# Moving first-level adds and norm transposes of a pre-norm transformer block onto DMA

## The chip, the cores and the metric

The kernel runs on one core of one Trainium2 chip. The metric is the device time of one execution in microseconds (us). A single execution scatters by about one per cent, so every variant was run several times, in rounds with the kernel before on the same chip. An execution is called fast when it is within 1.5% of the fastest of the same kernel; only fast ones enter the comparisons.

The engines are called PE (TensorE matmul), PEld (TensorE weight load, which overlaps PE), DVE (VectorE), ACT (ScalarE), POOL (GpSimd) and SP (SyncE). A name such as SPq means the engine's own instruction queue, from which it issues DMAs one after the other.

## The reference

One pre-norm block on 2048 rows of width 512: local dilated attention (32 heads of 16, eight shifts with a stride of two rows), then a gated ReLU feed-forward part (width 1376), each with a residual.

```python
def _A_ref(x, wqkv, wo):                 # H = 32, Dh = 16, W = 8, dil = 2
    q, k, v = ...(x @ wqkv)...           # each [B, H, S, Dh]
    idx = pos[:, None] - (jnp.arange(W) * dil)[None, :]
    kg, vg = k[..., idx, :], v[..., idx, :]
    logits = einsum("bhsd,bhswd->bhsw", q, kg) * Dh ** -0.5   # masked where idx < 0
    o = einsum("bhsw,bhswd->bhsd", softmax(logits), vg)       # the sum over eight shifts
    return merge_heads(o) @ wo

def _B_ref(x, W_gate, W_up, W_down):
    return (relu(x @ W_gate) * (x @ W_up)) @ W_down

h  = x + _A_ref(_layernorm(x), A_wqkv, A_wo)
out = h + _B_ref(_layernorm(h), B_W_gate, B_W_up, B_W_down)
```

## The kernel before

The 2048 rows are worked in four chunks (0 to 3) of 512 rows, each of four blocks of 128 rows. A chunk has two norms: the first (called x) feeds the q, k, v products, the second (called h) feeds the up and gate products. So there are eight norm outputs. Each is transposed before its products. A small planner in the kernel orders all operations: each has an engine, a planned duration, a planned extra latency and a rank from a tuned list, and every engine then executes its operations strictly in the planned order.

The parts that the change touches are these. A norm's output is transposed by TensorE, four 128x128 squares for a block, and ScalarE copies the result out of PSUM (the tiles called bank in the traces). A branch by DMA is there but not used:

```python
PESUM = ()
DMAT = ()                       # (norm, chunk) pairs to be transposed by DMA
RPE, OPE = (0,), ()             # chunk 0: attention residual added by TensorE (identity matmul)
...
if (ln, tk) in DMAT:
    for j in range(lo, hi):                 # a block of 128 rows
        xn, a = norm(j)
        def f_td(j=j, xn=xn):
            for t in range(NT):             # NT = 4 squares of 128x128
                nc.sync.dma_start_transpose(out=dst.t[:, t, j * P:(j + 1) * P],
                                            in_=xn.t[:, t * P:(t + 1) * P])
        evs.append(add((ln + "td" + gk, tk), "SP", 2.0, f_td, [a], pr,
                       take=[dst], use=[xn], lat=2.5))
    continue
...
def f_tp(j=j, j0=j0, xn=xn, tp=tp):         # the way by TensorE
    for t in range(NT):
        o = t * 2 * P + (j - j0) * P
        nc.tensor.transpose(tp.t[:].bitcast(BF16)[:, o:o + P],
                            xn.t[:, t * P:(t + 1) * P], identity[:])
```

The sum over the eight shifts is a tree on VectorE: eight weighted copies of v in one buffer, then halves are added three times.

```python
def f_a(n, mt):
    V.tensor_tensor(out=mt.t[:, 0:n, :], in0=mt.t[:, 0:n, :], in1=mt.t[:, n:2 * n, :], op=ALU.add)
...
m = add(("mu%d" % t, tk), "DVE", D40, f_mu, ...)      # the eight weighted copies
for n, du in ((4, D20), (2, D10), (1, D2)):
    f = lambda n=n, mt=mt, f=f_a: f(n, mt)
    if n == 1 and tk in EARLY: ...                    # last add writes the attention output
    else:
        m = add(("tree%d" % t, tk), "DVE", du, f, [m], tpr, use=[mt], lat=0.03)
```

The softmax here doesn't subtract the row's maximum and nothing guards it: scores larger than these inputs give would overflow.

## Time and profile before

| | before |
|---|---|
| time, median of 3 runs | 208.53 us (208.37 to 210.53) |
| span of the profiled execution | 206.6 us |
| TensorE, VectorE, ScalarE busy | 96%, 79%, 68% |
| GpSimd busy | 1% |

The page gives two more lines. The first is the clock that was granted to TensorE, in tenths, one digit for each fortieth of the span. The second is the chain of work that ended last, as shares of the span by engine.

```profile
PEclk9999999999999999999999999999999999999999
...
PE 64%; DVE 20%; issue 5%; DMA 4%; ACT 4%; SPq 1%; DVEq 0%
```

The clock never dips, and DMA hardly stands in the chain: only the first loads do. The timeline of SP at the start (start us, us, engine, line, operation, tile) has the row of issues. The last line is from the view of the stores' source line (issues in ns: least, median, most):

```profile
1.65 0.43 SPq L265 DMA_DIRECT2D wq_sb<-in_A_wqkv_dram  x1
2.12 0.51 SPq L265 DMA_DIRECT2D wv_sb<-in_A_wqkv_dram  x1
...
L773 SPq DMA_DIRECT2D out_dram<-row x17: 332/332/382, 103.1 to 204.3; - x17
```

These are plain copies from and to HBM, the chip's main memory. No transposing and no accumulating DMA runs in this kernel.

### The profile page before, as it was taken

The page shows a single profiled execution, that of the slowest core. Times are in us where ns is not written, and L with a number is a line of the kernel's source. Part 1 is how long each engine was busy: PE and PEld are TensorE (multiplying, and loading weights), DVE is VectorE, ACT ScalarE, POOL GpSimd, SP SyncE. Part 2 cuts the span into 40 slices and gives each one's busy share as a digit, 9 for nine tenths or more (in the row PEclk, how much of TensorE's full clock was granted, in tenths as well). Part 3 has the DMA queues.
Part 4 walks back from the last instruction along what each step waited for, and adds up shares of the span by engine and source line. Part 5 has one row for each costly group of instructions (what it writes and reads, how often), then busy time and mean ns, then how long its engine had stood idle before and what let it go on. Part 6 is the DMA issues. An engine that isn't in the chain of part 4 may idle for free.

```text
span 206.6 us, 2992 instructions
## 1 busy us (share of the span) xinstructions
PE 197.8 (96%) x1139; PEld 97.6 (47%) x1159; DVE 162.3 (79%) x241; ACT 140.6 (68%) x277; POOL 1.8 (1%) x14
## 2 busy tenths in 40 slices
PE   8697998999999999999999999999999999999994
PEld 8563444455543334444444444454444445444452
DVE  6579999999999999998889998659998564011414
ACT  3659989989899996749588557465465553535800
POOL 3000000000000000000000000000000000000000
PEclk9999999999999999999999999999999999999999
DMA  6999900000000000000010000001000000200003
GB/s 199 340 381 407 302 12 0 0 0 3 0 0 0 3 0 0 0 0 3 2 51 0 3 0 27 25 3 51 0 0 23 28 3 31 70 0 0 3 0 102
DMA packets 8813, 10.70 MB, mean 52 GB/s; under 512 B 512, under 2 KB 7648, under 8 KB 8800
## 3 DMA queue, kind: packets, MB, share of 16 engines
q1 hardware_dynamic: 7984, 9.73, 13.7%
q10 hardware_dynamic: 816, 0.79, 1.1%
q8 instruction: 9, 0.15, 0.3%
q14 instruction: 4, 0.03, 0.0%
HBM read 8.42 MB, written 2.10 MB: 51 GB/s over the span
## 4 chain that ended last, share of the span: by engine, by line
PE 64%; DVE 20%; issue 5%; DMA 4%; ACT 4%; SPq 1%; DVEq 0%
PE bank L721 37%; PE bank L758 19%; DVE big L549 7%; PE bank L683 5%; DMA x_sm<-in_A_x_dram 4%; DVE big L637 4%; DVE big L640 4%; DVE st L390 3%; ACT big L622 2%; PE bank L456 2%; ACT row L422 1%; PE bank L555 1%; ACT quad L510 1%; DVE quad L644 1%; PE bank L616 1%
## 5 line engine op out<-in xcount | busy, mean ns | idle before, releaser
L721 PE MATMUL bank<-quad,wu_sb 128*128 128x512 bf16 (+1 forms) x176 | 41.8, 379 | 0.1
L721 PE MATMUL bank<-quad,wg_sb 128*128 128x512 bf16 (+1 forms) x169 | 41.4, 379 | 0.3
L758 PE MATMUL bank<-wd_sb,gT 128*128 128x512 bf16 (+3 forms) x183 | 40.2, 366 | 0.2
L728 ACT ACTIVATE gr<-bank 128x512 bf16<-128x512 f32 (+1 forms) x44 | 25.8, 608 | 15.7 <-PE bank L721 10.9
L549 DVE TENSOR_TENSOR big<-quad,kT 128x4096 bf16<-128x4096 bf16 x16 | 35.9, 2279 | 0.1
L637 DVE TENSOR_TENSOR big<-big,vT 128x4096 bf16<-128x4096 bf16 x16 | 35.9, 2280 | 0.0
L725 ACT CAST up_sb<-bank 128x512 bf16<-128x512 f32 (+1 forms) x44 | 25.4, 589 | 14.3 <-PE bank L721 9.2
L640 DVE TENSOR_TENSOR big<-big 128x2048 bf16<-128x2048 bf16 (+2 forms) x36 | 30.5, 888 | 0.1
L741 DVE TENSOR_TENSOR gT<-gr,up_sb 128x1024 bf16<-128x1024 bf16 (+1 forms) x24 | 15.2, 639 | 18.4 <-ACT up_sb L725 11.6
L721 PEld LDWEIGHTS <-wg_sb 128*128 128x128 bf16 (+1 forms) x176 | 17.5, 100 | 20.6 <-issue 0.4
L721 PEld LDWEIGHTS <-wu_sb 128*128 128x128 bf16 (+1 forms) x176 | 17.5, 100 | 20.7 <-issue 0.8
L758 PEld LDWEIGHTS <-gT 128*128 128x128 bf16 (+1 forms) x187 | 17.8, 98 | 19.0 <-issue 0.9
L622 ACT CAST big<-bank 128x512 bf16<-128x512 f32 x32 | 16.8, 620 | 2.1 <-PE bank L616 2.1
L769 DVE TENSOR_TENSOR row<-x_sm,bank 128x512 bf16<-128x512 bf16 (+1 forms) x17 | 10.8, 653 | 9.4 <-PE bank L758 8.9
L470 ACT COPY quad<-bank 128x1024 bf16<-128x1024 bf16 (+1 forms) x16 | 15.2, 967 | 4.2 <-PE bank L456 3.9
L502 PE MATMUL bank<-quad,wv_sb 128*128 128x512 bf16 x61 | 15.9, 380 | 0.3 <-issue 0.2
L502 PE MATMUL bank<-quad,wq_sb 128*128 128x512 bf16 (+1 forms) x70 | 15.9, 355 | 0.1
L502 PE MATMUL bank<-quad,wk_sb 128*128 128x512 bf16 (+1 forms) x70 | 15.7, 355 | 0.1
L683 PE MATMUL bank<-wo_sb,quad 128*128 128x512 bf16 x62 | 15.0, 379 | 0.1
L360 ACT ACTIVATE row<-x_sm,mv 128x512 bf16<-128x512 bf16 x12 | 8.6, 718 | 8.1 <-DVE mv L352 7.8
L456 PE MATMUL bank<-identity,row 128*128 128x128 bf16 x128 | 10.2, 220 | 3.0 <-DVE row L425 1.8
L390 DVE BATCH_NORM_STATS2 st<-x_sm 128x6 f32<-128x512 bf16 x15 | 9.5, 679 | 3.9 <-DMA x_sm<-in_A_x_dram 3.9
(72 smaller groups left out, 165.5 us busy)
## 6 DMA issues: line engine op xcount, KB each, us to landing
out_dram<-row SPq DMA_DIRECT2D x15, 128.0 KB, 1.7
x_sm<-in_A_x_dram SPq DMA_DIRECT2D x3, 512.0 KB, 9.6
wu_sb<-in_B_W_up_dram SPq DMA_DIRECT2D x1, 1376.0 KB, 10.8
wg_sb<-in_B_W_gate_dram SPq DMA_DIRECT2D x1, 1376.0 KB, 13.4
wd_sb<-in_B_W_down_dram SPq DMA_DIRECT2D x1, 1280.0 KB, 15.6
wq_sb<-in_A_wqkv_dram SPq DMA_DIRECT2D x1, 512.0 KB, 6.4
wk_sb<-in_A_wqkv_dram ACTq DMA_DIRECT2D x1, 512.0 KB, 7.8
wv_sb<-in_A_wqkv_dram SPq DMA_DIRECT2D x1, 512.0 KB, 8.2
```

The lines of the kernel that those rows point to most:

```text
L390: V.bn_stats(out=st.t[:], in_=x_sm[:, tk * BPC + j, :])
L470: nc.scalar.copy(out=o, in_=i)
L502: nc.tensor.matmul(mm.t[:, lo:hi], lhsT=w3_sb[c][:, dt, t:D:NT], rhs=xnT.t[:, dt, lo:hi], start=(dt == 0), stop=(dt == NT - 1))
L549: V.tensor_tensor(out=pb.t[:].rearrange("p (t w) s -> p t w s", t=2), in0=q4, in1=k4, op=ALU.mult)
L622: nc.scalar.copy(out=ab.t[:, w, :], in_=bc.t[:])
L637: V.tensor_tensor(out=mt.t[:], in0=ab.t[:], in1=v8, op=ALU.mult)
L640: V.tensor_tensor(out=mt.t[:, 0:n, :], in0=mt.t[:, 0:n, :], in1=mt.t[:, n:2 * n, :], op=ALU.add)
L683: nc.tensor.matmul(od.t[:], lhsT=OT.t[:, t, j * P:(j + 1) * P], rhs=wo_sb[:, t, :], start=(t == 0), stop=(t == NT - 1 and tk not in RPE))
L721: nc.tensor.matmul(mm.t[:fs, :], lhsT=w_sb[:, dt, ft * P: ft * P + fs], rhs=hnT.t[:, dt, :], start=(dt == 0), stop=(dt == NT - 1))
L725: nc.scalar.copy(out=ub.t[:fs, i, :], in_=um.t[:fs, :])
L728: nc.scalar.activation(out=gr.t[:fs, i, :], in_=gm.t[:fs, :], func=ACT.Relu)
L758: nc.tensor.matmul(od.t[:, c0:c1], lhsT=gts[ft].t[:fs, ft % 2, j * P:(j + 1) * P], rhs=wd_sb[:fs, ft, c0:c1], start=(ft == 0), stop=(ft == ...
```

## The change

The intent is to take work off the two full engines. First, in chunks 0 to 2 the first and largest add of the tree becomes an accumulating DMA, issued by GpSimd: twelve of 512 KB. Second, five of the eight norm outputs (x of chunks 2 and 3, h of chunks 0, 1 and 2) take the branch by DMA: 20 blocks with four issues each, 80 issues of 32 KB on the SP queue. Third, chunk 0's residual goes back from TensorE to VectorE. Fourth, the list of ranks was tuned anew for the planner's durations, which book 2.0 us of SP and 2.5 us of latency for a block's four transposes.

```diff
 RANK = [
-    4, 1, 5, 2, 0, 3, 47, 6, 7, 29, 171, 229, 201, 272, 727, 10, 12, 8, 11, 14,
+    0, 1, 2, 3, 4, 5, 6, 7, 8, 9, 10, 11, 12, 13, 14, 17, 19, 15, 18, 22,
 ... (the rest of the list, all of it new, is cut)
     PESUM = ()
+
+    DACC = tuple((k, t) for k in range(3) for t in range(4))
+    DAL = 5.5
     NWARM = 48
-    DMAT = ()
+    DMAT = (("x",2),("x",3),("h",0),("h",1),("h",2))
 ...
-    RPE, OPE = (0,), ()
+    RPE, OPE = (), ()
 ...
             for n, du in ((4, D20), (2, D10), (1, D2)):
                 f = lambda n=n, mt=mt, f=f_a: f(n, mt)
+                if n == 4 and (tk, t) in DACC:
+                    def f_da(mt=mt):
+                        nc.gpsimd.dma_start(mt.t[:, 0:4, :], mt.t[:, 4:8, :], accum_op=ALU.add)
+
+                    m = add(("ta%d" % t, tk), "POOL", 1.5, f_da, [m], tpr, use=[mt], lat=DAL)
+                    continue
```

## The prediction

> **What bounds the kernel now.** I read four views of the kernel before: the page's busy shares and slices, the busy times of stretches, the chain that ended last in order of time, and the groups by shape. First the page:
>
> ```profile
> PE 197.8 (96%) x1139; PEld 97.6 (47%) x1159; DVE 162.3 (79%) x241; ACT 140.6 (68%) x277; POOL 1.8 (1%) x14
> ...
> PE   8697998999999999999999999999999999999994
> ...
> DVE  6579999999999999998889998659998564011414
> ```
>
> TensorE looks busy everywhere, so taking work from it should pay one for one. But VectorE shows nines from slice 4 to 18. So two engines look full at once, and the page doesn't say which one sets the time. The stretches (columns: start:end, length, then busy us and instructions of PE, PEld, DVE, ACT, POOL, the clock, DMA share, GB/s) give it by stage:
>
> ```profile
> 12.00:69.80 57.80, 55.24 (x359) 26.40 (x364) 57.66 (x73) 52.87 (x107) 0.00 (x0) 1.00 0.24 88
> 72.05:203.90 131.85, 131.03 (x666) 61.52 (x679) 95.77 (x143) 78.92 (x152) 0.00 (x0) 1.00 0.04 15
> ```
>
> From 12 to 69.8 us VectorE idles 0.14 us in 57.8. After that it is 73% busy and TensorE has no gaps. The chain (start, us, what) says the same:
>
> ```profile
> 37.98 6.68 DVE big L637 x3
> 44.67 1.14 DVE big L640
> 45.80 0.07 DVE nb L411
> 45.88 2.27 DVE big L640 x2
> 48.15 2.20 DVE big L637
> 50.35 4.27 DVE big L640 x8
> ...
> 69.79 2.21 DVE big L549
> 72.00 0.04 issue
> 72.05 0.61 PE bank L555 x8
> ```
>
> Until about 72 us the kernel waits for VectorE's attention of chunk 0, its residual, norm and transposes; from the first matmuls of the feed-forward part it waits for TensorE alone. Three groups by shape size what is removed, and one line of the DMA view is the only small transfer to go by:
>
> ```profile
> L456 PE MATMUL bank<-identity,row 128*128 128x128 bf16 x128 | 10.2, 220 | 3.0 <-DVE row L425 1.8 <-ACT row L422 1.1
> L640 DVE TENSOR_TENSOR big<-big 128x2048 bf16<-128x2048 bf16 x16 | 18.9, 1214 | 0.0
> L692 ACT ACTIVATE x_sm<-bank 128x512 bf16<-128x512 f32 x4 | 2.4, 614 | 0.0
> ```
>
> ```profile
> out_dram<-row SPq DMA_DIRECT2D x15, 128.0 KB, 1.7
> ```
>
> A mean of 220 ns isn't what a transpose costs: they overlap. The timeline has 16 transposes in 0.90 us (0.0565 us each) and 8 feed-forward matmuls in 1.73 us (0.2165 each).
>
> **What the Trainium skill says.** "DMA: Bandwidth & Descriptors", section "Anatomy of one DMA", puts a GpSimd-issued DMA at about 2.0 us plus its bytes at 436 GB/s. The trace has no such DMA; its 1.7 us for 128 KB from the SP queue is near that. The same page, "Rules for kernel authors", says that DMA transposes come from SP or ACT and accumulation from GpSimd, as the change has it; no run shows either yet. "SBUF — State Buffer", section "Who interferes with whom", says that descriptor generation on GpSimd is locked out by VectorE's two-port modes but infers that tensor_tensor leaves the write port free; most of VectorE's time here is tensor_tensor, so I expect no long lock-out. "TensorE: Matmul & The Clock Gate", "What's actually happening", halves the clock after an idle window of about 3.4 us; before, the granted clock is 0.998 and there is no such gap.
>
> **The change part by part.** I compare the two programs' orders of instructions on each engine.
>
> TensorE loses 80 of 128 transposes: 80 x 0.0565 = 4.5 us. It also loses the 4 identity matmuls that added chunk 0's residual (4 x 0.2165 = 0.9). Counting all matmuls at their spacings, its work falls from 195.7 to 190.3 us: 5.4 us, 2.6% of the span. This is the most that the TensorE view promises.
>
> ScalarE loses ten evacuations of 128x1024 (ten at about 0.95 = 9.5 us) and four residual evacuations (2.4). It is no bound; the attention weights of chunk 0 just arrive earlier.
>
> VectorE loses 12 first-level adds (12 x 1.14 = 13.7 us by spacing) and gains 4 residual adds (0.69 each, 2.8 us). Only chunk 0's share lies before the turning point: minus 4.6, plus 2.8.
>
> GpSimd gains 12 accumulating DMAs of 512 KB, SP 80 transposes of 32 KB.
>
> Now the path. The output projection of chunk 0 needs all of that chunk's attention. At 29.1 us both programs have done the same VectorE work (12 statistics, 12 aggregates, 4 score products, 2 masks). Before, the next 27.4 us (to 56.5) bring that attention. In the new order, what stands between is 4 score products and 4 weight products (8 x 2.22 = 17.8), 4 second-level adds (4 x 0.60), 4 last adds and 4 scalings (8 x 0.34) and one small one: 23.0 us. So it is ready at 52.1, 4.4 us earlier.
>
> But what TensorE has issued by then counts. In the old order 50.4 us of its work stands before the first projection matmul, in the new one 41.3: the filler has moved behind it. TensorE will wait there; I put the waits at about 5 us, in three places (two score reductions and the projection). What is left after it is 145.3 us before and 190.3 - 41.3 = 149.1 after. Before, those 145.3 took 147.0 (56.84 to 203.8, by the chain), 1.2% more. So after: 52.1 + 149.1 x 1.01 = 202.7 at the end of TensorE, against 203.8.
>
> A second gate: the feed-forward part waits for chunk 0's norm, now transposed by DMA. VectorE's sum to the last of its four rows is the old 69.7 - 4.6 + 2.8 = 67.9, plus some 0.6 of waiting for the projection, 68.5. Four issues of about 0.45 us (what SP took per issue at the start of the trace) and 2 us of landing give 72.5, about where the matmuls arrive anyway (52.1 + 61.8 - 41.3 = 72.7). Before, four transposes and an evacuation took from 69.7 to 72.4. So the transposes by DMA take nothing from this path and add about 1.5 us to it. Later chunks have 15 us of other matmuls between projection and feed-forward part, by the new order, so they hide theirs.
>
> Chunk 1's projection: VectorE's rows to it sum to about 88.8 us, TensorE gets there at 87.8, one more us lost. Sum: 202.7 + 1.0 + the 2.8 us tail (residual add and store as before) = 206.5 us of span, and 1.9 between span and time as before: 208.4. **With no DMA wait this is 207 to 208.5 us.**
>
> What of the accumulations? In the new order VectorE's next touch of the same buffer comes 9.1, 7.9, 9.4 and 7.7 us after the product in chunk 0, and some 7 to 9 in chunks 1 and 2. An estimate from the skill's fit, counting source and destination as read (1 MB): 2.0 + 2.4 = 4.4 us. The kernel's own plan books 1.5 + 5.5. Either fits. But products come every 2.22 us, four in a row, so the transfers queue: at T each, the fourth lands about 2 + 4T after the first product. It is wanted 6.7 + 7.7 = 14.4 after it. So T up to about 3.1 us is hidden; the estimate of 2.4 fits with little room.
>
> **The rivals.**
> One: the whole 5.4 us come out (span 201.2, time 203.1). For it: TensorE's 96%. Against: the chain before 72 us holds VectorE, and its sum can't give the projection before 52; even with no loss after that, 52.1 + 149.1 + 2.8 + 1.9 = 205.9.
> Two: accumulating DMAs run at half the rate hoped (T near 4 to 5 us). Then VectorE, in order, waits 4 to 7 us in chunk 0, as much in chunk 1, and the TensorE behind it too: 213 to 220 us. For it: read-modify-write in memory, queueing in fours, no measured rate in this trace. Against: the DMA engines are otherwise idle after 26 us (slices at 0), and the read ahead is generous.
> Three: transposes are slow to issue or land (twice my 4 us): the second gate moves by 3 to 4 us: 211 to 212. Against it: 32 KB each and an idle queue.
> Four: TensorE's new waits near 42 to 52 us reach a clock window; each costs a few us of half speed, about 210. For it: 3 us in one place, close to the limit. Against: warm work on both sides.
> Five: everything is hidden and the later gates vanish, with 206 to 207.
>
> **Range and chances.** The middle case has 208.4; its lower edge is the VectorE sum, 205.9, which makes faster by over 2% (below 204.4) nearly impossible unless instructions get shorter. Upwards there are rivals two to four, together some one in three, of which two thirds would pass 212.7. So I put the middle slightly up at 208.6, the range at 206.4 to 215.0, chances 0.03 faster, 0.75 same, 0.22 slower.
>
> **What would show it.** Right: PE busy near 192 us, VectorE near 152; gaps on TensorE between 40 and 53 us put down to the score products or the projection's input; chunk 0's projection starting at 51 to 54 us and the first feed-forward matmul at 72 to 74; VectorE's second-level adds not waiting for a DMA; transposes landing in 2 to 3 us. Wrong: second-level adds with idle time put down to accumulating DMAs (rival two), a landing time above 9 us, feed-forward matmuls waiting for the transposed tile (three), a granted clock below 0.98 after 15 us (four), or a projection before 50 us, which would break my sum of VectorE's work.

## The result, and the profile after

The changed kernel took **278.46 us**, median of four fast runs (277.36 to 279.16). The kernel before had 209.17 us in the same rounds (208.37 to 210.53). Ratios in this document are the mean time of one kernel's fast runs over that of the other's in the same rounds, so they aren't quite the ratio of these medians. Here it is 1.330 (95% interval 1.321 to 1.339): a third slower, where the prediction had 208.6 us. The result was correct.

The page of the kernel after has these lines in answer to those of before (busy us and shares; busy tenths and clock in 40 slices; the chain by engine; two groups, with count, busy us, mean ns and the idle time before them with what ended it; two kinds of DMA, with count, KB of each and median us from issue to landing):

```profile
PE 206.8 (75%) x1075; PEld 93.8 (34%) x1075; DVE 152.5 (55%) x237; ACT 128.9 (47%) x259; POOL 12.3 (4%) x26
...
PE   6789950189629940699997029999807999999995
...
PEclk9999995569957995599999757999975999999999
...
PE 46%; SPq 19%; DVE 16%; ACT 8%; DMA 8%; issue 3%; DVEq 0%; ACTq 0%
...
L730 PE MATMUL bank<-quad,wu_sb 128*128 128x512 bf16 (+1 forms) x176 | 48.0, 415 | 27.5 <-DMA quad<-row 27.5
...
L505 PE MATMUL bank<-quad,wq_sb 128*128 128x512 bf16 (+1 forms) x72 | 20.1, 404 | 25.7 <-DMA quad<-row 24.1
...
L643 DVE TENSOR_TENSOR big<-big 128x1024 bf16<-128x1024 bf16 (+2 forms) x24 | 16.9, 732 | 0.4 <-DMA big<-big 0.4
...
big<-big POOLq DMA_DIRECT2D x12, 512.0 KB, 6.3
...
quad<-row SPq DMA_TRANSPOSE x80, 2.4
```

Read from the top. No engine is full any more. TensorE has five holes (the low digits of its slices), and the clock dips at or just after each of them. A queue, SPq, has come into the chain with 19%. The groups name the tile that TensorE waited for: quad<-row, the transposed norm outputs. The second-level adds (L643) waited 0.4 us for the accumulating DMAs (big<-big), which is nothing. And the last line is a trap: from issue to landing a transpose takes 2.4 us, just as the prediction's list of signs had it. (This time counts from the start of the issue.)

So where are 70 us? The timeline of TensorE has the holes, in brackets at the end of each line, and shows chunk 0's output projection (L692) between them:

```profile
52.62 0.62 PE L505 MATMUL bank<-quad,wq_sb 128*128 128x512 bf16 x1 [13.89 <-DMA quad<-row]
...
67.15 3.62 PE L692 MATMUL bank<-wo_sb,quad 128*128 128x512 bf16 x16
...
79.74 0.62 PE L505 MATMUL bank<-quad,wq_sb 128*128 128x512 bf16 x1 [6.27 <-DMA quad<-row]
...
111.93 1.44 PE L730 MATMUL bank<-quad,wu_sb 128*128 128x512 bf16 x3 [12.71 <-DMA quad<-row]
...
161.79 0.59 PE L730 MATMUL bank<-quad,wu_sb 128*128 128x512 bf16 x1 [12.18 <-DMA quad<-row]
...
205.61 0.58 PE L730 MATMUL bank<-quad,wg_sb 128*128 128x512 bf16 x1 [6.89 <-DMA quad<-row]
...
206.84 0.58 PE L730 MATMUL bank<-quad,wg_sb 128*128 128x512 bf16 x1 [0.64 <-DMA quad<-row]
```

There is one hole for each norm output that is transposed by DMA: x of chunks 2 and 3 (q products), then h of chunks 0, 1 and 2 (up or gate products). They sum to 51.9 us. After four of the five, TensorE goes on at a matmul every 1.25 us or so, as the last line shows: it is fed square by square.

The transposes are in the view of their one source line: duration of the issue in ns (least, median, most), then the time from the start of the issue to landing.

```profile
L445 SPq DMA_TRANSPOSE quad<-row x80: 1094/1230/2961, 28.2 to 207.0; - x80
...
DMA to landing us min/median/max: 2.2/2.4/8.7
```

A single issue keeps the SP queue for **1.23 us**, nearly three times the 0.43 us of the plain copy above, and for nearly 3 us at worst. The queue issues one at a time. Four issues for each of four blocks make 16 x 1.27 us (with the 0.04 us between them) = 20.3 us for one chunk's norm, at the least. The chain of waits has them one behind the other (start us, us), up to the last square of chunk 2's x, which lands at 54.01 + 2.37 = 56.38 us:

```profile
41.84 2.39 SPq L445
...
44.27 2.74 SPq L445
...
47.06 2.96 SPq L445
...
54.01 2.37 DMA quad<-row
```

The long ones here (2.4 to 3.0 us) lie beside accumulating DMAs of chunk 0, whose packets the trace has from 38.7 to 50.7 us.

### The profile page after: what moved, and what is told of

Read it like the earlier page. It is cut to its first block, busy times and chain, and to the rows that moved or that the text cites. A ratio compares the mean times of both kernels' runs of the same rounds, so it can differ in the third digit from the quotient of the medians.

```text
span 275.6 us, 3015 instructions
## 1 busy us (share of the span) xinstructions
PE 206.8 (75%) x1075; PEld 93.8 (34%) x1075; DVE 152.5 (55%) x237; ACT 128.9 (47%) x259; POOL 12.3 (4%) x26
## 3 DMA queue, kind: packets, MB, share of 16 engines
q0 software_dynamic: 1728, 6.29, 12.5%
## 4 chain that ended last, share of the span: by engine, by line
PE 46%; SPq 19%; DVE 16%; ACT 8%; DMA 8%; issue 3%; DVEq 0%; ACTq 0%
PE bank L730 26%; SPq L445 18%; PE bank L767 8%; DVE big L640 6%; PE bank L505 5%; DMA quad<-row 4%; PE bank L692 4%; DMA x_sm<-in_A_x_dram 4%; ACT big L625 4%; DVE big L552 3%; DVE big L643 2%; DVE st L393 2%; ACT row L425 1%; DVE x_sm L703 1%; ACT kT L513 1%
## 5 line engine op out<-in xcount | busy, mean ns | idle before, releaser
L730 PE MATMUL bank<-quad,wu_sb 128*128 128x512 bf16 (+1 forms) x176 | 48.0, 415 | 27.5 <-DMA quad<-row 27.5
L730 PE MATMUL bank<-quad,wg_sb 128*128 128x512 bf16 (+1 forms) x176 | 44.1, 386 | 8.9 <-DMA quad<-row 8.9
L505 PE MATMUL bank<-quad,wq_sb 128*128 128x512 bf16 (+1 forms) x72 | 20.1, 404 | 25.7 <-DMA quad<-row 24.1
L513 ACT CAST quad<-bank 128x512 bf16<-128x512 f32 x16 | 9.5, 593 | 25.5 <-PE bank L505 25.5
L505 PEld LDWEIGHTS <-wq_sb 128*128 128x128 bf16 x72 | 7.9, 118 | 36.5 <-DMA quad<-row 28.1
L778 DVE TENSOR_TENSOR row<-x_sm,bank 128x512 bf16<-128x512 bf16 (+1 forms) x17 | 10.9, 653 | 16.6 <-PE bank L767 16.5
L643 DVE TENSOR_TENSOR big<-big 128x1024 bf16<-128x1024 bf16 (+2 forms) x24 | 16.9, 732 | 0.4 <-DMA big<-big 0.4
L505 PE MATMUL bank<-quad,wk_sb 128*128 128x512 bf16 (+1 forms) x72 | 17.0, 378 | 0.0
L672 POOL DMA_DIRECT2D big<-big x12 | 10.5, 873 | 140.6 <-DVE big L640 139.0
L703 DVE SCALAR_TENSOR_TENSOR x_sm<-x_sm,bank 128x512 bf16<-128x512 bf16 x16 | 11.0, 688 | 8.4 <-PE bank L692 8.0
L428 DVE TENSOR_SCALAR row<-x_sm,mv,rs 128x512 bf16<-128x512 bf16 x20 | 7.4, 410 | 13.8 <-ACT rs L410 13.8
```

The costliest lines, as they stand in the source:

```text
L505: nc.tensor.matmul(mm.t[:, lo:hi], lhsT=w3_sb[c][:, dt, t:D:NT], rhs=xnT.t[:, dt, lo:hi], start=(dt == 0), stop=(dt == NT - 1))
L703: V.scalar_tensor_tensor(out=r, in0=r, scalar=1.0, in1=od.t[:], op0=ALU.mult, op1=ALU.add, accum_out=sm.t[:, j:j + 1])
L730: nc.tensor.matmul(mm.t[:fs, :], lhsT=w_sb[:, dt, ft * P: ft * P + fs], rhs=hnT.t[:, dt, :], start=(dt == 0), stop=(dt == NT - 1))
```

## The experiments

Two theories were set against each other at first. **Queue**: the loss comes from the number of issues of transposing DMAs, each of which holds the SP queue. **Accumulation**: the accumulating DMAs fill the DMA engines or hold the buffers, and the transposes are only the place where that is seen. A third, weaker one was that the new **order** is bad by itself. Later runs asked what each part is worth once the issues are few. Twelve variants ran; all gave a correct result. The times are medians of fast and, where a variant had any, slower runs; the ratios use fast runs alone. By the traces, e1 and f1 keep the change's order on TensorE, and e4 that of the kernel before; in e2, e3, f2 and g2 the planner moved some operations, so a difference to these contains that too.

| run | what it is | time, us | ratio to before (95%) |
|---|---|---|---|
| the change | 4 issues a block, accumulation | 278.46 | 1.330 (1.321 to 1.339) |
| e1_one_issue | the change, 1 issue a block | **207.76** | 0.992 (0.988 to 0.997) |
| f1_two_issues | the change, 2 issues a block | 222.05 | 1.053 (1.047 to 1.060) |
| e2_no_acc | the change without accumulation | 274.33 | 1.310 (1.303 to 1.317) |
| f2_one_no_acc | 1 issue, no accumulation | 220.30 | 1.054 (1.050 to 1.059) |
| e3_no_trans | the change without transposes by DMA | 213.36 | 1.022 (1.016 to 1.027) |
| e4_acc_before | before's ranks, accumulation alone | 208.54 | 0.997 (0.993 to 1.001) |
| f3_before_h12 | before's ranks, h of chunks 1, 2 by 1 issue | 217.82 | 1.043 (1.038 to 1.047) |
| f4_before_acc_h12 | f3 and accumulation | 214.86 | 1.028 (1.023 to 1.032) |
| g3_strict_h12 | f3 in before's exact order | 213.12 | 1.019 (1.015 to 1.024) |
| g1_replanned | e1 with ranks searched anew | 211.26 | 1.010 (1.005 to 1.014) |
| g1b_replanned | g1, and chunk 3 accumulates too | 215.73 | 1.031 (1.028 to 1.035) |
| g2_honest80 | the change, planner told 5.08 us a block | 261.72 | 1.255 (1.249 to 1.260) |

### One issue for a block instead of four (e1)

```diff
-for t in range(NT):
-    nc.sync.dma_start_transpose(out=dst.t[:, t, j * P:(j + 1) * P],
-                                in_=xn.t[:, t * P:(t + 1) * P])
+nc.sync.dma_start_transpose(out=dst.t[:, :, j * P:(j + 1) * P], in_=xn.t[:])
```

The same bytes go to the same places, the planned durations are left alone, and so the order on every engine is the same. Only the number of issues falls, from 80 to 20.

> The changed kernel with the same order of instructions, but each block's four 128x128 transposes issued as one transpose of 128x512: 20 issues instead of 80, the same bytes. Theory A (a fixed cost per issued transpose, 1.23 us median in the changed kernel): the queue needs some 5 us a chunk instead of 20, TensorE's 60 us of waiting for the transposed tile fall below 8 us, time 207 to 216 us. Theory B (the cost goes with the bytes or the small tiles moved): one issue takes 4 to 5 us, TensorE still waits over 50 us, time 270 to 282 us.

It took 207.76 us: the whole loss is gone, and 0.8% besides. Its page and the view of the line of the transposes:

```profile
PE 192.5 (94%) x1056; PEld 92.4 (45%) x1075; DVE 151.3 (74%) x237; ACT 128.0 (62%) x259; POOL 12.3 (6%) x26
```

```profile
L444 SPq DMA_TRANSPOSE quad<-row x20: 1188/1216/1303, 27.2 to 133.6; - x20
...
DMA to landing us min/median/max: 2.4/2.4/4.3
```

An issue of 128 KB takes the queue as long as one of 32 KB: 1.22 against 1.23 us. **The price is for the issue, not for the bytes.** None is longer than 1.3 us here. The accumulating DMAs still run, but at other times: the trace has their packets from 37.8 to 48.8, 74.0 to 86.2 and 105.7 to 117.5 us, and only one transpose (at 48.0 us) was issued in these stretches. The bytes of payload moved and the time from issue to landing (2.4 us) are those of the changed kernel; neither can be the cause.

The timeline of TensorE is now that of the prediction (projection of chunk 0, first up product, projection of chunk 1):

```profile
51.88 3.63 PE L690 MATMUL bank<-wo_sb,quad 128*128 128x512 bf16 x16 [0.94 <-DVE quad L645]
...
72.83 3.62 PE L728 MATMUL bank<-quad,wu_sb 128*128 128x512 bf16 x15
...
88.75 1.47 PE L690 MATMUL bank<-wo_sb,quad 128*128 128x512 bf16 x6 [0.21 <-DVE quad L664]
```

The two kernels let the loss be counted. The spans differ by 275.6 - 205.2 = 70.4 us. TensorE's waits for transposed tiles in the changed kernel sum to 36.5 (up and gate) + 24.1 (q) = 60.6 us. The other 10 us are slower matmuls: TensorE was busy 206.8 us against 192.5, and as e1's trace lacks 19 of 1075 matmul records, worth about 19 x 0.2165 = 4.1 us by estimate, against 196.6. In the changed kernel the granted clock was 0.62 from 39.0 to 52.6 us, where TensorE had nothing to do, and 0.81 from 52.6 to 70 us, where it ran again.

### Two issues for a block (f1)

```diff
-for t in range(NT):
-    nc.sync.dma_start_transpose(out=dst.t[:, t, ...], in_=xn.t[:, t * P:(t + 1) * P])
+for t in range(0, NT, 2):
+    nc.sync.dma_start_transpose(out=dst.t[:, t:t + 2, ...], in_=xn.t[:, t * P:(t + 2) * P])
```

> The changed kernel, same order, each block's transposes in two issues of 128x256: 40 issues, the same bytes, half-way between 80 and 20. Theory A (about 1.22 us per issue whatever its size): a chunk's queue needs 10 us; the first and third of the five transposed chunks hold TensorE some us each, the others are hidden; 211 to 224 us, issue again 1.2 us each. If the cost had a part by size, an issue would differ from 1.2 us, as neither the 32 KB nor the 128 KB ones did.

It took 222.05 us (220.2 over its two fast executions), ratio 1.053, between one issue and four. The profile fell in an execution classed as slow, so only the issue is read from it:

```profile
L445 SPq DMA_TRANSPOSE quad<-row x40: 1168/1216/2667, 27.5 to 154.3; - x40
```

At 64 KB the issue takes 1.22 us as well: three sizes, one price. A chunk's norm holds the queue for about 5, 10 and 20 us with one, two and four issues a block. Above the time of e1 that costs 0, some 12.5 and 71 us. It isn't proportional; that would fit TensorE having other work for the first microseconds of each wait and none for the rest.

### Without the accumulations (e2)

```diff
-    DACC = tuple((k, t) for k in range(3) for t in range(4))
+    DACC = ()
```

> The changed kernel with the first-level adds back on VectorE: transposes by DMA alone. Theories A and B: the transposes still take 1.23 us each to issue, only those that ran beside accumulating DMAs (2 to 3 us each) get shorter, time 258 to 275 us. Theory C (transposes are slow because the accumulating DMAs load the same engines): issue well under 1 us each and time below 230 us.

It took 274.33 us. The issues still had a median of 1.23 us, and TensorE waited 29.4 + 22.7 us for transposed tiles.

```profile
L445 SPq DMA_TRANSPOSE quad<-row x80: 1094/1230/2196, 27.8 to 203.6; - x80
```

The theory of accumulation falls: taking all of it away gives back 2 of 33 per cent. It does make single issues longer: the longest here was 2.2 us, against 3.0 with it.

### Without the transposes by DMA, and accumulation alone (e3, e4)

```diff
 e3, from the change                          e4, from the kernel before
-    DMAT = (("x",2), ... ("h",2))            +    DACC = tuple((k, t) for k in range(3) ...)
+    DMAT = ()                                +    (and the branch f_da of the change)
```

The transposes of e3 take their place in the changed kernel's order beside the operations they belong to. Its residual is on VectorE, as in the change; that of e4 is on TensorE, as before.

> The changed kernel with all norm outputs transposed by TensorE again: accumulating DMAs alone. If the loss is all from the transposes (A, B or C): 205 to 211 us, accumulations landing within 6 to 7 us and VectorE waiting for them under 2 us in sum. Theory D (the accumulations cost time by themselves): above 216 us with VectorE's second-level adds waiting for them.

> The kernel before, its own priorities, with only the first-level adds of chunks 0 to 2 moved to accumulating DMAs. VectorE's busy time falls by 13 to 14 us. If TensorE is the bound after 72 us and only the path through chunk 0's attention can shorten: 204 to 208 us. If the accumulations are a cause of loss (D): above 213 us.

e3 took 213.36 us and e4 208.54. So the new order with its transposes put back on TensorE loses 2.2%, and e1 gains 5.6 us over it: that is about what quick transposes by DMA are worth here (moved operations included), where the prediction counted 4.5 us of TensorE's time for them. In the old order the accumulations are worth nothing certain (0.3%, interval 0.993 to 1.001), though VectorE's busy time fell from 162.3 to 150.9 us: that part of VectorE's time isn't on the path that sets the end. e3 fell between its two expected ranges, and e4 just above the 204 to 208 us expected. In e4 the wait that the accumulations make is small too, as its view of waits shows (total us, times, longest):

```profile
DVE big L643 <- DMA big<-big: 3.1, 2, 2.1
```

### One issue, no accumulation (f2)

The edits are those of e1 and e2 together.

> The one-issue kernel with the first-level adds of all chunks back on VectorE. If VectorE's sum sets the start of chunk 0's output projection (51.9 us with accumulating DMAs), four adds of 1.14 us put it at 56 to 57 us and the whole time moves by 3 to 5 us: 210.5 to 213.5 us. If the accumulations bring nothing there (the rival: VectorE is not on the path once transposes are quick), 206 to 209 us.

It took 220.30 us, 12.5 more than e1, and missed both expected ranges. That is more than the 3 to 5 us which one chunk's adds (4.6 us) on the path would cost. The timeline of TensorE shows where it goes:

```profile
56.85 3.63 PE L690 MATMUL bank<-wo_sb,quad 128*128 128x512 bf16 x16 [0.86 <-DVE quad L645]
...
99.01 3.61 PE L690 MATMUL bank<-wo_sb,quad 128*128 128x512 bf16 x16 [0.31 <-ACT gr L735]
```

Chunk 0's projection comes 5.0 us after that of e1, about one chunk's adds. Chunk 1's comes 10.9 us after it (in e1 its first matmul was at 88.16 us): a second chunk's adds are on VectorE's path by then, and VectorE was busy for 41.93 of the 42 us from 57 to 99. So the accumulations are worth 0.3% in the old order and some 6% in the new one, whose operations were ranked to count on them; the operations that the planner moved in f2 are in the 6%.

### The transposes of chunks 1 and 2 alone, in the old order (f3, f4, g3)

The prediction said that later chunks hide their transposes behind other matmuls. f3 has before's ranks, and only h of chunks 1 and 2 by DMA with one issue a block. f4 adds the accumulations. In both the planner moved many other operations, because their planned times changed. g3 therefore adds a rule to the planner that lets each engine take only the head of before's exact order:

```diff
-    DMAT = ()
+    DMAT = (("h",1),("h",2))
 g3 also:
+    head = {}
+    for op in waiting:
+        if op.eng not in head or (op.prio, op.seq) < head[op.eng]:
+            head[op.eng] = (op.prio, op.seq)
+    best = {e: [c for c in cs if (c[1].prio, c[1].seq) == head[e]] for e, cs in best.items()}
```

> The kernel before with its own priorities, and only the second norms of chunks 1 and 2 transposed by DMA, one issue per block: 8 issues in all, each with 15 us of other matmuls behind which to hide. TensorE is the bound there and loses 32 transposes of 0.0565 us, 1.8 us. If those are hidden: 206 to 208 us against 209.3. If the new wait on the transposed tile shows: 209 to 212 us.

> The same, and the first-level adds of chunks 0 to 2 by accumulating DMA. The accumulations alone in the old order were worth 0.3 percent, so 205.5 to 208 us if both parts add up; 209 or more if they hinder each other on the DMA engines.

> The kernel before with its exact order on every engine; only the second norms of chunks 1 and 2 transposed by DMA, one issue per block, in place of TensorE's transposes and ScalarE's evacuations at the same point. TensorE saves 1.8 us. In the old order its next use of the tile comes 3.6 us after the last norm row, and four issues with landing take over 5 from the first row: it should wait some 2 to 3 us at each of the two places. 209.5 to 213 us. If the transposes were hidden after all, 207 to 208.5.

f3 was a miss: 217.82 us. TensorE waited only 1.9 us for a transposed tile there; the rest came with the new order, in which chunk 3's products were pulled forward and VectorE carried the chain from 107 to 150 us. f3 doesn't tell what the transposes cost, and f4 (214.86, also a miss) shares its fault. g3 does, with 213.12 us, just above its expected range. Its timeline of TensorE has the two places:

```profile
112.20 3.28 PE L734 MATMUL bank<-quad,wg_sb 128*128 128x512 bf16 x8 [2.78 <-DMA quad<-row]
...
147.97 1.02 PE L734 MATMUL bank<-quad,wg_sb 128*128 128x512 bf16 x4 [1.82 <-DMA quad<-row]
```

32 transposes by TensorE are saved (32 x 0.0565 = 1.8 us), and 4.6 us of waits come in. That is 2.8 us of the 4 lost; the rest isn't accounted for (the granted clock was 0.984 over the span, but some runs of the kernel before had that too). In an order that was tuned for TensorE's transposes even one quick issue a block loses. This suggests that what the transposes by DMA are worth depends on how much other work stands between norm and product.

### A plan that knows the price (g1, g1b, g2)

```diff
 g2, from the change:
-  add((ln + "td" + gk, tk), "SP", 2.0,  f_td, [a], pr, take=[dst], use=[xn], lat=2.5)
+  add((ln + "td" + gk, tk), "SP", 5.08, f_td, [a], pr, take=[dst], use=[xn], lat=1.4)
 g1: as e1, with "SP", 1.27 and lat=1.4, and new ranks from a search over the kernel's own plan
 g1b: as g1, with its own search, and
-    DACC = tuple((k, t) for k in range(3) for t in range(4))
+    DACC = tuple((k, t) for k in range(4) for t in range(4))
```

> The changed kernel with its 80 issues and its priorities, but the plan told that a block's four issues hold the queue for 5.08 us instead of 2.0, so that it puts other work of TensorE where the transposed tile isn't there yet. The queue still needs 80 times 1.27, 102 us. If only the wrong booking was at fault: below 215 us. If the queue itself is the limit (the first transposed chunks have nothing else for TensorE to do): 230 to 255 us, with TensorE still waiting for the transposed tile.

> The one-issue kernel (same operations) with the plan told what an issue costs (1.27 us on the queue, landing 1.4 later) and priorities chosen anew by a search over the kernel's own plan. If the one-issue kernel's remaining loss lies in the order (TensorE waiting 4 us in three places before and at the first output projection), 204 to 207 us against its 207.8 and 209.3 before; if the order doesn't matter any more, 207 to 209.

> As the last, and chunk 3's first-level adds by accumulating DMA too. VectorE has slack at that stage, so the same time within 1 us: 204 to 207 us.

g2 keeps the 80 issues but the planner knows that a block holds the queue for 4 x 1.27 us. It took 261.72 us, more than the 230 to 255 expected of a queue that is the limit. So a plan with the true price gets back 17 of 70 us, though with ranks that were tuned for the wrong one. No search for new ranks with 80 issues was run, so how much the best order could hide stays open. The waits (total us, times, longest) have spread:

```profile
ACT row L363 <- DMA quad<-row: 18.7, 1, 18.7
...
PE bank L558 <- DVE big L552: 17.6, 3, 7.1
PE bank L730 <- DMA quad<-row: 17.2, 10, 6.3
```

The first is ScalarE waiting for a row buffer that the slow transposes still hold.

g1 should have improved on e1, and was slower than it by 3.5 us (211.26). g1b was slower still. Both searches took the planned durations as fixed and, it seems, used up the slack around the transposes. The plan booked 1.27 us for an issue and 1.4 more for landing. On the chip an issue took up to 2.4 us in g1 and 3.5 us in g1b, and from its start to landing up to 5.0 and 7.7 us, these two beside accumulating DMAs. The longest waits ended with these slowest landings. First the landing and products of chunk 2's q in g1, then the landing and up products in g1b:

```profile
36.86 5.01 DMA quad<-row
...
42.12 1.87 PE L527 MATMUL bank<-quad,wq_sb 128*128 128x512 bf16 x4 [4.64 <-DMA quad<-row]
```

```profile
137.32 7.69 DMA quad<-row
...
145.15 3.57 PE L752 MATMUL bank<-quad,wu_sb 128*128 128x512 bf16 x8 [6.31 <-DMA quad<-row]
```

A plan without slack is worth less than its own figure says. The best kernel is e1, 0.8% faster than the kernel before (interval 0.3 to 1.2%).

## Why the prediction was wrong, and where it was right

The predicted time was 208.6 us in a range of 206.4 to 215.0; 278.46 was measured. Its own steps, in order:

- **What bounds the kernel, and the path through VectorE: right.** With quick transposes (e1) the projection started at 51.9 us (said: 52.1), the first up product at 72.8 (72.7), and chunk 1's projection had its wait for VectorE end at 88.75 (88.8). The time of 207.76 lies in the "207 to 208.5 us" which the prediction gave for no DMA wait. VectorE's busy time was 151.3 (said: near 152). The prediction described e1, not the kernel it was given: it allowed a block 3.8 us for its transposes, and e1's one issue takes 2.4 with landing. (A slip in its sum, 68.5 + 3.8 = 72.3 and not 72.5, changed nothing.)
- **The accumulations are hidden: right.** VectorE waited 0.4 us for them in the changed kernel. From issue to landing one took 6.3 us, in e1 6.1; the condition that the prediction set for it ("T up to about 3.1 us") was not overstepped: the packets of the first four ran for 11.0 us in e1, 2.75 each. Rival two is out.
- **The failing step: "Four issues of about 0.45 us (what SP took per issue at the start of the trace) and 2 us of landing".** The issue was mis-sized by a factor of 2.7: it took 1.23 us, and the 0.45 came from plain copies, another kind. The landing was not too short: 2.4 us from the start of the issue are 1.2 after its end, where 2 were said. The 3.8 us of that sum become 3 x 1.27 + 2.4 = 6.2 us, if the queue is empty.
- **The second fault of the same step: the queue isn't empty.** It counted only the last block's issues. With 0.45 us a chunk's sixteen would take 7 us; with 1.27 they take 20.3 us, so three blocks stand in front of the last one. The first up product of chunk 0 came at 111.9 us, not 72.7, the delay of the next point included.
- **A gate was left out: x of chunks 2 and 3.** The prediction worked out chunk 0's h and waved the later h through ("15 us of other matmuls"). It never asked what the q products of chunks 2 and 3 wait for, and the first hole (13.9 us, at 39 to 52 us) is there, ahead of the projection, which then came at 67.2 us instead of 52.1. The 15 us themselves would not have been enough against 20.
- **Rival three was the mechanism, with the wrong size.** It named "slow to issue or land" and even what would show it ("feed-forward matmuls waiting for the transposed tile"). It gave 3 to 4 us in one place. The runs showed 60.6 us of waits in all. "Against it: 32 KB each and an idle queue" was the weak argument: the size in KB has no part in the price, as 32, 64 and 128 KB show.
- **Rival four came on top.** The holes are long enough for the clock to fall, as the section of the Trainium skill that the prediction cites for it ("TensorE: Matmul & The Clock Gate", "What's actually happening") has it: 0.62 in the hole, 0.81 after it, some 10 us by the count above. The count rests on estimated missing records; no run isolates the clock from the holes that cause it.

What the Trainium skill has on this could have misled as well. "Advanced Engine Details and Errata", section "X-Bar Transpose (TRN2)", says that "TRN2 transpose DMAs are as fast as regular DMAs". The trace agrees for what follows the end of an issue (2.4 - 1.2 = 1.2 us for 32 or 128 KB, against 1.7 - 0.33 = 1.4 for a plain store of 128 KB), and disagrees for the issue itself (1.22 us against 0.33, both for 128 KB), which is what bounded this kernel.

Two things stay open. Chunk 0's residual on VectorE was not tried alone. And the transposes were not spread over two queues: the skill's "DMA: Bandwidth & Descriptors", section "Silent corruption: two transposing streams in flight at once", says that two such streams at once can spoil both results, and no run here tests it.

## What to carry to other kernels

Here a transposing DMA held its queue for 1.2 us an issue, whatever its size, and a plain store of 128 KB for 0.33; beside other DMAs an issue could take twice as long or more. Before moving work to a queue, multiply the price of its kind by all issues in front of the one that is needed, and compare the sum with the work that covers it. Merge small transposes into one issue with a wider access pattern (here 4 into 1, worth 70 us), and measure an unknown kind of issue in a one-line variant before trusting a price taken from another kind. An offloaded operation is worth what the order makes of it: the same accumulations were worth 0.3% in one order and some 6% in the other.

## What the Trainium skill lacked or had wrong

- "DMA: Bandwidth & Descriptors", section "DMA Transpose (X-bar)": lists constraints and other ways, but no price of an issue in time for a transpose between SBUF tiles. (The page's part on trn3 B0 has counts in cycles for unnamed "previous generations".) The runs show 1.22 to 1.23 us on the SP queue, for 32, 64 and 128 KB alike, against 0.33 us for a plain store of 128 KB, and a landing 2.4 us after the start of the issue.
- "Advanced Engine Details and Errata", section "X-Bar Transpose (TRN2)": "as fast as regular DMAs" leaves out the issue, which took 1.22 us against 0.33 for a plain store of the same 128 KB. With 80 issues of 32 KB the kernel was 33% slower, with 20 of 128 KB 0.8% faster.
- No page that I found has it: a transpose's issue takes longer beside certain other DMAs. In the traces of the eleven runs with transposes by DMA, 304 issues overlap no packet of the accumulations or of the two instruction queues that the profile's page lists (q8, q14), and none of these took over 1.31 us. All 57 longer ones overlap one: 43 accumulations (up to 3.5 us, in g1b), 14 the instruction queues alone (up to 2.4 us). Why isn't known.
- "DMA: Bandwidth & Descriptors", section "Anatomy of one DMA": its fit, with source and destination both counted as read, gave the prediction 4.4 us for an accumulation of 512 KB within SBUF. That is near the 4.5 to 5.0 us which the first of each four took from issue to landing in e1; the fit says nothing of several in flight, and the median was 6.1 us there, the longest 7.3.
- "SBUF — State Buffer", section "Who interferes with whom": the inference that tensor_tensor doesn't lock out descriptor generation is not contradicted: GpSimd's issues took 0.86 us beside a full VectorE.
